# The head of a fused layer norm, S5 and GEGLU kernel: one tile leads the layer norm, weights arrive in other chunks on one queue, and TensorE gets dummies in between

## The chip, the cores and the metric

The kernel runs on one core of a Trainium2 chip. The metric is device time in microseconds (us).

## The reference

The input is normalised without a learned scale, then goes through two branches in parallel: a diagonal state space (S5) with a skip, and a GEGLU feed-forward. Input, branches and skip are added.

```python
B, S, D, F, P = 1, 2048, 512, 1376, 512          # bf16 inputs and output
xn = (x - mean(x)) / sqrt(var(x) + 1e-5)
# branch A: h[t] = Lam_bar * h[t-1] + B_bar @ xn[t] (complex, 512 states);  y = 2 Re(C h) + xn * Dskip
# branch B: (gelu(xn @ w_gate) * (xn @ w_up)) @ w_down
return x + A(xn) + B(xn)
```

## The kernel before

The 2048 tokens are four blocks (0 to 3) of four tiles of 128 tokens. The feed-forward's 1376 hidden columns are eleven column tiles (ten of 128, one of 96). The program is a list of operations with the buffers they read and write. A list scheduler fixes each engine's order from estimated durations and inserts semaphore waits; TensorE and the SyncE queue keep the order in which the operations were written. A change of an estimate can thus reorder VectorE and ScalarE anywhere.

Five names recur. `LN` normalises (VectorE, with a small Sqrt on ScalarE in block 0). `TR0` transposes a tile of block 0 on TensorE through PSUM and evicts it. `GU` is gate and up. `BU` is the state input. `DN` is the output product.

```python
nwarm = 11                                    # dummies: 128x512 matmuls on zeros, so that the array comes to full clock
PE(fwarm, ...)
LN(0, [0, 1], True)                           # tiles 0 and 1 as a pair
TR0(0, "AV")                                  # two transposes evicted by ScalarE, two by VectorE
TR0(1, "V", ...)
LN(0, [2, 3], True, ...)
load_B()
GU_first(range(5), range(3), hbanks)          # gate/up of column tiles 0..4 on block 0, piece by piece
...
BU(0); CHAIN(0, 2); SKIP(0); LN(1); SKIP(1); TR(1); load_C()
GU(0, [5, 10, 6, 7, 8, 9])
# ... blocks 1 to 3 likewise, then DN(2), DN(3)

FCH = [(0, 384), (384, 896), (896, F)]        # weight chunks: 3, 4 and 4 column tiles
for j in range(4): ld_x0(j)                   # SyncE queue
ld_w(WG, ..., 0, "scalar")                    # w_gate chunk 0, ScalarE queue
ld_w(WU, ..., 0); ld_w(WG, ..., 1); ld_w(WU, ..., 1)

# GU_first, TensorE order: early = column tiles 0, 1, 2
for n in (1, 0):
    for ft in early: mm(ft, 0, 0, 1, [2*n, 2*n+1], ...)   # gate, tile 0, 128 columns a matmul
for ft in early: mm(ft, 1, 0, 1)                          # up, tile 0
params()                                                   # one tiny transpose
for ft in early:
    for u in range(2): mm(ft, u, 1, 2)                    # gate and up, tile 1
mm(late[0], 0, 0, 2)                                      # gate of column tile 3, tiles 0 and 1: 256 columns
TR0(2, "V"); TR0(3, "A")
# ... evictions; gate of column tile 4, up of 3 and 4 (256 columns); then tiles 2 and 3 of all five
```

## Time and profile before

| | before |
|---|---|
| time, median | 179.52 us (3 runs, 179.49 to 179.67) |
| execution of the profile | 179.44 us, span 177.6 |
| TensorE, VectorE, ScalarE busy | 98%, 88%, 52% |
| first gate matmul | 6.45 us |
| first matmul of BU(0) | 16.10 us in the list; 16.26 on the chain, behind the end of GU |
| end of the last matmul | 175.35 us |

From the page of before: the span, the busy time of each engine, the granted clock of TensorE in 40 slices, and the shares of the chain of work that ended last.

```profile
span 177.6 us, 2525 instructions
...
PE 173.5 (98%) x927; PEld 86.4 (49%) x927; DVE 156.3 (88%) x275; ACT 91.5 (52%) x175; POOL 10.1 (6%) x20
...
PEclk9999999999999999999999999999999999999999
...
PE 95%; DVE 2%; DMA 1%; issue 0%; ACT 0%; ACTq 0%; DVEq 0%
```

The PEclk row is what a throttle grants.

The same chain in order of time (start, length, what), for its first 16 us:

```profile
2.87 1.29 DVE arena L603 x2
...
5.11 0.42 DVE arena L615
...
5.58 0.41 PE PS L640 x4
...
6.45 0.83 PE PS L729 x12
7.28 0.03 issue
7.30 0.84 PE PS L729 x12
...
16.26 6.91 PE PS L667 x32
```

After 6.45 us the chain is matmuls. The 3.6 us from the arrival of tile 0 to the first gate matmul are the only long stretch in which another engine decides.

The timeline restricted to TensorE's matmuls (start, length, line, how many; merged when back to back). L889 are dummies, L640 transposes, L729 the first gate and up, L537 the tiny transpose, L667 BU.

```profile
0.99 3.88 PE L889 MATMUL PS<-arena 128*128 128x512 bf16 x11 [0.99 <-DVE arena L515]
5.58 0.72 PE L640 MATMUL PS<-arena 128*128 128x128 bf16 x8 [0.70 <-DVE arena L615]
6.45 1.70 PE L729 MATMUL PS<-arena 128*128 128x128 bf16 x24
8.08 0.18 PE L537 MATMUL PS<-arena 12*128 12x12 bf16 x1
8.19 1.95 PE L729 MATMUL PS<-arena 128*128 128x128 bf16 x28
9.98 0.61 PE L640 MATMUL PS<-arena 128*128 128x128 bf16 x8
10.42 5.84 PE L729 MATMUL PS<-arena 128*128 128x256 bf16 x52
16.10 7.07 PE L667 MATMUL PS<-arena 128*128 128x512 bf16 x32
```

The same for weight loads, one ahead of each matmul. Their spacing shows the array's clock:

```profile
3.10 0.15 PEld L889 LDWEIGHTS PS<-arena 128*128 128x128 bf16 x1 [0.28 <-issue]
3.52 0.15 PEld L889 LDWEIGHTS PS<-arena 128*128 128x128 bf16 x1 [0.28 <-issue]
3.85 0.53 PEld L889 LDWEIGHTS PS<-arena 128*128 128x128 bf16 x3 [0.17 <-issue]
...
7.30 0.67 PEld L729 LDWEIGHTS PS<-arena 128*128 128x128 bf16 x12 [0.20 <-DMA arena<-in_B_w_up_dram]
```

Up to 3.52 the loads are 0.43 us apart, then 0.21: the array came to full clock near 3.7 us in this execution. At 7.30 the load waited for the first chunk of w_up.

### The profile page before, as it was taken

Reading aid. Unit: us, or ns where it says so; the run is one execution under the profiler, and the core shown is the slowest. Engines: PE = TensorE matmul, PEld = TensorE weight load, DVE = VectorE, ACT = ScalarE, POOL = GpSimd, SP = SyncE. Lnnn points to the kernel's source line nnn. Section 1 sums busy time; section 2 is a strip of 40 time slices with the busy share of each in tenths; the row PEclk is TensorE's granted clock in tenths of the full one; section 3 lists DMA queues with packets and bytes.
Section 4 is the critical chain, followed back from the end, with each engine's and each line's share of the span. In section 5 each row is a group of like instructions: output and inputs, shape, how many; then the busy total and the mean of one; then the engine's idle time right before and its main releaser. Section 6 shows DMA issues by size and latency. Waiting matters only on the chain.

```text
span 177.6 us, 2525 instructions
## 1 busy us (share of the span) xinstructions
PE 173.5 (98%) x927; PEld 86.4 (49%) x927; DVE 156.3 (88%) x275; ACT 91.5 (52%) x175; POOL 10.1 (6%) x20
## 2 busy tenths in 40 slices
PE   7899999999999999999999999999999999999994
PEld 2597464444644444444644444444464444444453
DVE  5759997998998999779999999999999999999311
ACT  3289999976766899002576495000658700620000
POOL 3120025000000002400000000000000000000000
PEclk9999999999999999999999999999999999999999
DMA  4999914999043000001015000000001000002211
GB/s 132 336 302 163 327 26 95 194 159 339 13 86 61 4 0 0 0 30 63 30 33 113 3 6 0 30 30 30 30 4 30 0 0 0 0 0 78 73 50 39
DMA packets 26387, 12.90 MB, mean 73 GB/s; under 512 B 17704, under 2 KB 26376, under 8 KB 26376
## 3 DMA queue, kind: packets, MB, share of 16 engines
q1 hardware_dynamic: 25824, 12.36, 28.3%
q10 hardware_dynamic: 552, 0.40, 0.9%
q8 instruction: 7, 0.11, 0.3%
q14 instruction: 4, 0.03, 0.1%
HBM read 6.46 MB, written 2.10 MB: 48 GB/s over the span
## 4 chain that ended last, share of the span: by engine, by line
PE 95%; DVE 2%; DMA 1%; issue 0%; ACT 0%; ACTq 0%; DVEq 0%
PE PS L846 37%; PE PS L806 34%; PE PS L667 16%; PE PS L729 5%; PE PS L780 3%; DMA arena<-in_A_x_dram 1%; DVE arena L603 1%; PE PS L640 0%; DVE arena L615 0%; ACT arena L607 0%; DVE arena L649 0%; DVE arena L864 0%; DVE arena L604 0%; DVE arena L611 0%; PE PS L537 0%
## 5 line engine op out<-in xcount | busy, mean ns | idle before, releaser
L846 PE MATMUL PS<-arena 128*128 128x512 bf16 (+3 forms) x323 | 66.2, 366 | 0.0
L806 PE MATMUL PS<-arena 128*128 128x512 bf16 x280 | 61.7, 379 | 0.0
L846 PEld LDWEIGHTS PS<-arena 128*128 128x128 bf16 (+1 forms) x323 | 30.8, 98 | 35.2
L821 ACT ACTIVATE arena<-PS 128x512 bf16<-128x512 f32 x35 | 20.8, 598 | 46.4 <-PE PS L806 33.0
L806 PEld LDWEIGHTS PS<-arena 128*128 128x128 bf16 x280 | 27.3, 98 | 32.1
L700 DVE TENSOR_TENSOR_SCAN arena<-arena 128x512 bf16<-128x512 f32 x32 | 38.8, 1253 | 0.0
L667 PE MATMUL PS<-arena 128*128 128x512 bf16 x128 | 28.3, 379 | 0.0
L824 ACT ACTIVATE arena<-PS 128x512 bf16<-128x512 f32 x35 | 20.8, 597 | 4.9 <-PE PS L806 4.9
L667 PEld LDWEIGHTS PS<-arena 128*128 128x128 bf16 x128 | 12.5, 98 | 14.9
L864 DVE TENSOR_TENSOR arena<-PS,arena 128x512 bf16<-128x512 f32 (+2 forms) x17 | 10.9, 651 | 9.6 <-PE PS L846 9.6
L671 ACT ACTIVATE arena<-PS 128x512 bf16<-128x512 f32 x32 | 17.7, 597 | 3.0 <-PE PS L667 2.9
L826 DVE TENSOR_TENSOR arena<-arena 128x512 bf16<-128x512 bf16 x35 | 13.7, 416 | 2.9 <-ACT arena L824 2.9
L838 ACT ACTIVATE PS<-arena 128x512 f32<-128x512 bf16 (+2 forms) x17 | 9.6, 581 | 5.5 <-DVE arena L864 4.8
L603 DVE BATCH_NORM_STATS2 arena<-arena 128x6 f32<-128x512 bf16 x16 | 10.1, 680 | 1.2 <-DMA arena<-in_A_x_dram 1.1
L729 PE MATMUL PS<-arena 128*128 128x256 bf16 (+1 forms) x104 | 9.5, 248 | 0.2
L687 DVE TENSOR_TENSOR arena<-arena 128x4096 bf16<-128x4096 bf16 (+1 forms) x5 | 9.3, 1857 | 0.0
L689 DVE TENSOR_TENSOR arena<-arena 128x4096 bf16<-128x4096 bf16 (+1 forms) x5 | 9.3, 1856 | 0.0
L712 DVE TENSOR_TENSOR arena<-arena 128x4096 bf16<-128x4096 bf16 x4 | 9.1, 2286 | 0.0
L713 DVE TENSOR_TENSOR arena<-arena 128x4096 bf16<-128x4096 bf16 x4 | 9.1, 2286 | 0.0
L729 PEld LDWEIGHTS PS<-arena 128*128 128x128 bf16 x104 | 8.1, 98 | 1.1 <-issue 0.3
L622 DVE TENSOR_TENSOR arena<-arena 128x512 bf16<-128x512 bf16 x16 | 6.0, 414 | 0.0
L780 PE MATMUL PS<-arena 128*128 128x192 bf16 x64 | 5.9, 246 | 0.0
(84 smaller groups left out, 106.5 us busy)
## 6 DMA issues: line engine op xcount, KB each, us to landing
out_dram<-arena SPq DMA_DIRECT2D x15, 128.0 KB, 1.7
arena<-in_A_x_dram SPq DMA_DIRECT2D x3, 512.0 KB, 7.3
arena<-in_B_w_down_dram SPq DMA_DIRECT2D x1, 1280.0 KB, 6.9
arena<-in_A_x_dram SPq DMA_DIRECT2D x4, 128.0 KB, 3.0
arena<-in_B_w_gate_dram SPq DMA_DIRECT2D x1, 512.0 KB, 6.1
arena<-in_B_w_up_dram SPq DMA_DIRECT2D x1, 512.0 KB, 7.0
arena<-in_B_w_gate_dram SPq DMA_DIRECT2D x1, 480.0 KB, 4.4
arena<-in_B_w_up_dram SPq DMA_DIRECT2D x1, 480.0 KB, 5.6
```

The lines of the kernel that those rows point to most:

```text
L603: V(lambda e, tt=tt: e.bn_stats(ST[tt].ap, X[tt].ap), d_dve_1x(512), [X[tt]], [ST[tt]], "bnst", after)
L667: ins_ = e.matmul(PS[bank][:, :], BBT[c][dk].ap[:, 128 * s:128 * (s + 1)], XNT[b].ap[:, dk, :], start=(dk == 0), stop=(dk == KD - 1))
L671: ACT(lambda e, bank=bank, k3=k3, s=s, c=c: e.activation(SSc[k3][s][c].ap, PS[bank][:, :], ACTF.Copy), d_act(512), [BANK[bank]], [SSc[k3][ ...
L700: V(lambda e, g=g, rb=rb, init=init: e.tensor_tensor_scan(g.ap, rb, g.ap, init, ALU.mult, ALU.add), d_dve_scan(512), [g, PA[RRr]] + ([CARc ...
L729: ins_ = e.matmul(PS[bank][:, q0:q0 + 128 * (j1 - j0)], W.ap[:, dk, 128 * ft:128 * (ft + 1)], XNT[0].ap[:, dk, 128 * j0:128 * j1], start=( ...
L780: ins_ = e.matmul(dst, XNT[b].ap[:, dk, 128 * j:128 * (j + 1)], WGU[:, :, dk, f0:f0 + m], start=(dk == 0), stop=(dk == KD - 1))
L806: ins_ = e.matmul(PS[bank][0:m, c0:c1], W.ap[:, dk, 128 * ft:128 * ft + m], XNT[b].ap[:, dk, c0:c1], start=(dk == 0), stop=(dk == KD - 1))
L821: GATE["last_gelu"] = ACT(lambda e, bg=bg, kk=kk, m=m: e.activation(GG[kk].ap[0:m, :], PS[bg][0:m, :], ACTF.Gelu_apprx_tanh), d_act(512), ...
L824: ACT(lambda e, bu=bu, kk=kk, m=m: e.activation(UPB[kk].ap[0:m, :], PS[bu][0:m, :], ACTF.Copy), d_act(512), [BANK[bu]], [UPB[kk]], "evU")
L826: V(lambda e, kk=kk, m=m, ft=ft, k2=k2: e.tensor_tensor(HTt[k2][ft].ap[0:m, :], GG[kk].ap[0:m, :], UPB[kk].ap[0:m, :], ALU.mult), d_dve_tt ...
L846: ins_ = e.matmul(PS[bank][:, c0:c1], l_[:, 128 * j:128 * (j + 1)], r_[:, c0:c1], start=False, stop=last and n == len(ops) - 1, skip_group ...
L864: V(lambda e: e.tensor_tensor(OUTB[ko].ap[:, c0:c1], PS[bank][:, c0:c1], XD[tt].ap[:, c0:c1], ALU.add), d_dve_1x(c1 - c0), [BANK[bank], XD ...
```

## The change

The intent is to start real TensorE work earlier and keep it fed. Tile 0 is normalised ahead of tile 1, and three small dummies fill the gap between their transposes. The weight chunks are 3, 2 and 6 column tiles, all on the SyncE queue in the order of need. The up of column tiles 0 to 2 waits until tile 1 is there and runs in 256-column matmuls. The last evictions of GU_first let VectorE read PSUM. Block 1's LN goes in pairs. The last DN does the hidden products of two tiles ahead of the states. The scheduler gets other estimates. The core of the diff:

```diff
-        FCH = [(0, 384), (384, 896), (896, F)]
+        FCH = [(0, 384), (384, 640), (640, F)]
...
-        for j in range(4):
-            ld_x0(j)
-        ld_w(WG, WGc, ins["B_w_gate"], 0, "scalar").nb = 900.0
+        ld_x0(0)
+        ld_x0(1)
+        ld_w(WG, WGc, ins["B_w_gate"], 0)
+        S.dma(... X_all.ap[:, 2:4, :] ...)          # tiles 2 and 3 in one transfer
         ld_w(WU, WUc, ins["B_w_up"], 0)
...
-        wchunk = lambda ft: 0 if ft < 3 else (1 if ft < 7 else 2)
+        wchunk = lambda ft: 0 if ft < 3 else (1 if ft < 5 else 2)
...
+        def LN_first():                              # fixed VectorE order, one tile at a time
+            for step, j in ((stats, 0), (aggr, 0), (stats, 1), (recip, 0), (aggr, 1), (norm, 0), (recip, 1), (norm, 1)):
+                step(j)
...
+                if h and ft >= 3:                    # VectorE multiplies straight from PSUM
+                    up, rd, dur = PS[bank][:, 256:512], BANK[bank], d_dve_1x(256)
...
-            for n in (1, 0):
+            for n in range(2):
                 for ft in early:
-                    mm(ft, 0, 0, 1, [2 * n, 2 * n + 1], 2, 1, [XT0h[n]])
+                    mm(ft, 0, 0, 1, [2 * n, 2 * n + 1], toks=[XT0h[n]])
             for ft in early:
-                mm(ft, 1, 0, 1)
+                mm(ft, 0, 1, 2)
             params()
             for ft in early:
-                for u in range(2):
-                    mm(ft, u, 1, 2)
+                mm(ft, 1, 0, 2)
             late = [ft for ft in fts if ft not in early]
-            mm(late[0], 0, 0, 2)
+            for ft in late:
+                mm(ft, 0, 0, 2)
             TR0(2, "V")
             TR0(3, "A")
...
+            elif tail:                               # DN(3)
+                for j in range(2):
+                    seed(j); hidden(j)
+                for j in range(2):
+                    states(j); store(j)
...
-        nwarm = 11
+        nwarm = 10
...
-        LN(0, [0, 1], True)
-        TR0(0, "AV")
+        LN_first()
+        TR0(0, "AA")
+        fill(3)
...
-        LN(1); SKIP(1)
+        LN(1, [0, 1]); LN(1, [2, 3]); SKIP(1)
```

More of the change, by code (lines that the diff above doesn't have):

```diff
@@ L16 @@
 SELF_LAT = 40.0
-LAT = lambda d, op: SYNC_LAT if d.kind == "dma" or d.eng != op.eng else (0.0 if d.eng == "tensor" else SELF_LAT)
+LAT = lambda d, op: SYNC_LAT if d.kind == "dma" or d.eng != op.eng else (0.0 if d.eng == "tensor" or d is op.behind else SELF_LAT)
 DMA_ISSUE = 500.0
@@ L63 @@
     __slots__ = ("id", "eng", "fn", "dur", "deps", "kind", "reads", "writes", "start", "finish",
-                 "sem", "val", "users", "tag", "issue", "nb")
+                 "sem", "val", "users", "tag", "issue", "nb", "behind")
     def __init__(self, id_, eng, fn, dur, kind, reads, writes, tag):
@@ L74, in __init__ @@
         self.nb = 0.0
+        self.behind = None
 class Sched:
@@ L125, in dma, with order_behind @@
             self.out_ops.append(op)
+        return op
+    def order_behind(self, op, prev):
+        if prev is not None and prev not in op.deps:
+            op.behind = prev
+            op.deps.append(prev)
+            prev.users.append(op)
         return op
@@ L268, in _forward @@
                 xfer = op.dur - 2000.0
-                t0 = max(st, dma_pipe)
-                dma_pipe = t0 + xfer
+                t0 = max(st, dma_pipe) if xfer > 10.0 else st
+                dma_pipe = max(dma_pipe, t0 + xfer)
                 op.finish = t0 + xfer + 2000.0
@@ L308, in emit @@
                 for d in op.deps:
-                    if d.kind == "eng" and d.eng == e and e == "tensor":
+                    if d.kind == "eng" and d.eng == e and (e == "tensor" or d is op.behind):
                         continue
@@ L471, in ld_x0 @@
             S.dma(lambda e, j=j: e.dma_start(X[j].ap, x2[128 * j:128 * (j + 1), :]), 128 * 1024, writes=[X[j]], tag="ld_x0")
-        for j in range(4):
-            ld_x0(j)
-        ld_w(WG, WGc, ins["B_w_gate"], 0, "scalar").nb = 900.0
+        ld_x0(0)
+        ld_x0(1)
+        ld_w(WG, WGc, ins["B_w_gate"], 0)
+        S.dma(lambda e: e.dma_start(X_all.ap[:, 2:4, :], x2[256:512, :].rearrange("(j p) d -> p j d", p=128)),
+              256 * 1024, writes=X[2:4], tag="ld_x0")
         ld_w(WU, WUc, ins["B_w_up"], 0)
@@ L477, in build @@
         ld_w(WU, WUc, ins["B_w_up"], 1)
-        for q, nm in enumerate(("A_log_dt", "A_Lambda_re", "A_Lambda_im")):
+        for q, (nm, nb) in enumerate((("A_log_dt", 0.0), ("A_Lambda_re", 500.0), ("A_Lambda_im", 1000.0))):
             S.dma(lambda e, q=q, nm=nm: e.dma_start(PROW.ap[4 * q:4 * q + 4, :], ins[nm].rearrange("(s p) -> s p", p=128)),
-                  1024, writes=[PROWq[q]], tag="ld_" + nm, queue="scalar")
+                  1024, writes=[PROWq[q]], tag="ld_" + nm, queue="scalar").nb = nb
         def late_loads():
@@ L519, in build @@
         SCR = A.alloc("SCR", [1], F32)
-        ACT(lambda e: e.activation(SCR.ap, HALF.ap[:, 0:1], ACTF.Sqrt), 200, [HALF], [SCR], "sqrt0").nb = 1900.0
+        ACT(lambda e: e.activation(SCR.ap, HALF.ap[:, 0:1], ACTF.Sqrt), 200, [HALF], [SCR], "sqrt0").nb = 1600.0
         POOL(lambda e: e.memset(HR.ap, 0.0), 300, [], HRp, "hr0")
@@ L582, in build, with tables_dve @@
         K1s, F1s = ring(K1, "K1", KP), ring(F1, "F1", KP)
-        def tables_dve():
+        def tables_dve(behind):
             for s in range(KP):
@@ L589, in tables_dve @@
                   d_dve_1x(512), [IOTJ, W16p[0], K1s[s]], [F1s[s]], "f1")
-            V(lambda e: e.tensor_scalar(A1.ap.bitcast(I32), F1.ap.bitcast(I32), 0x7FFFFFFF, None, ALU.bitwise_and), d_dve_ts4x(2048) * 2, F1s, [A1], "a1")
+            S.order_behind(V(lambda e: e.tensor_scalar(A1.ap.bitcast(I32), F1.ap.bitcast(I32), 0x7FFFFFFF, None, ALU.bitwise_and), d_dve_ts4x(2048) * 2, F1s, [A1], "a1"), behind)
         def tables_act(after_gelu):
@@ L595, in tables_act, with dve, stats, aggr @@
             return ACT(lambda e: e.activation(SINT.ap, F1.ap, ACTF.Sin, scale=-SIN_SCALE), d_act(2048), [F1], [SINT], "sint", after=[t])
+        def LN_first():
+            mvs = [MVt[0][j] for j in range(2)]
+            mns, qbs, rqs = ([cols(t, 0, j, j + 1) for j in range(2)] for t in (MN, QB, RQ))
+            last = [None]
+            def dve(*args):
+                last[0] = S.order_behind(V(*args), last[0])
+            def stats(j):
+                dve(lambda e: e.bn_stats(ST[j].ap, X[j].ap), d_dve_1x(512), [X[j]], [ST[j]], "bnst")
+            def aggr(j):
+                dve(lambda e: e.bn_aggr(mvs[j].ap, ST[j].ap), D_TINY, [ST[j]], [mvs[j]], "bnag")
+                POOL(lambda e: e.tensor_copy(mns[j].ap, mvs[j].ap[:, 0:1]), 200, [mvs[j]], [mns[j]], "mn")
+                ACT(lambda e: e.activation(qbs[j].ap, mvs[j].ap[:, 1:2], ACTF.Sqrt, bias=EPS.ap), d_act(4),
+                    [mvs[j], EPS, SCR], [qbs[j]], "sqrt")
+            def recip(j):
+                dve(lambda e: e.reciprocal(rqs[j].ap, qbs[j].ap), 150, [qbs[j]], [rqs[j]], "rq")
+            def norm(j):
+                dve(lambda e: e.tensor_scalar(XN[j].ap, X[j].ap, mns[j].ap, rqs[j].ap, ALU.subtract, ALU.mult),
+                    d_dve_ts4x(512), [X[j], mns[j], rqs[j]], [XN[j]], "ln_n")
+            for step, j in ((stats, 0), (aggr, 0), (stats, 1), (recip, 0), (aggr, 1), (norm, 0), (recip, 1), (norm, 1)):
+                step(j)
         def LN(b, js=range(4), on_act=False, after=()):
@@ L606, in LN @@
             if on_act:
-                ACT(lambda e: e.activation(qb.ap, mv.ap[:, :, 1], ACTF.Sqrt, bias=EPS.ap), d_act(4), [mv, EPS, SCR], [qb], "sqrt")
+                GATE["sqrt"] = ACT(lambda e: e.activation(qb.ap, mv.ap[:, :, 1], ACTF.Sqrt, bias=EPS.ap), d_act(4),
+                                   [mv, EPS, SCR], [qb], "sqrt")
             else:
@@ L611, in LN @@
             V(lambda e: e.reciprocal(rq.ap, qb.ap), 150, [qb], [rq], "rq")
+            last = None
             for j in js:
@@ L614, in LN @@
                 xs = XN[tt % 8]
-                V(lambda e, tt=tt, j=j, xs=xs: e.tensor_scalar(
+                last = S.order_behind(V(lambda e, tt=tt, j=j, xs=xs: e.tensor_scalar(
                     xs.ap, X[tt].ap, mn.ap[:, j - j0:j - j0 + 1], rq.ap[:, j - j0:j - j0 + 1], ALU.subtract, ALU.mult),
-                  d_dve_ts4x(512), [X[tt], mn, rq], [xs], "ln_n")
+                  d_dve_ts4x(512), [X[tt], mn, rq], [xs], "ln_n"), last)
+            return last
         def SKIP(b):
@@ L656, in TR @@
                     XNT[b].ap[:, :, 128 * j:128 * (j + 1)], XN[tt % 8].ap),
-                    1.2 * 128 * 1024, reads=[XN[tt % 8]], writes=[XTk[b][j]], tag="tr_x%d" % b)
+                    3.0 * 128 * 1024, reads=[XN[tt % 8]], writes=[XTk[b][j]], tag="tr_x%d" % b, issue=1280.0)
         def BU(b):
@@ L719, in GU_first, with mm @@
         def GU_first(fts, early, banks):
-            def mm(ft, u, j0, j1, dks=range(KD), first=0, last=KD - 1, toks=None):
+            def mm(ft, u, j0, j1, dks=range(KD), toks=None):
                 W, Wc = ((WG, WGc), (WU, WUc))[u]
@@ L729, in f @@
                         ins_ = e.matmul(PS[bank][:, q0:q0 + 128 * (j1 - j0)], W.ap[:, dk, 128 * ft:128 * (ft + 1)],
-                                        XNT[0].ap[:, dk, 128 * j0:128 * j1], start=(dk == first), stop=(dk == last))
+                                        XNT[0].ap[:, dk, 128 * j0:128 * j1], start=(dk == 0), stop=(dk == KD - 1))
                     return ins_
@@ L738, in evac @@
                                         d_act(256), [BANK[bank]], [GG[kk]], "gelu", after)
-                ACT(lambda e: e.activation(UPB[kk].ap[:, 0:256], PS[bank][:, 256:512], ACTF.Copy),
-                    d_act(256), [BANK[bank]], [UPB[kk]], "evU")
-                V(lambda e: e.tensor_tensor(HTt[0][ft].ap[:, c0:c0 + 256], GG[kk].ap[:, 0:256], UPB[kk].ap[:, 0:256], ALU.mult),
-                  d_dve_tt2x(256), [GG[kk], UPB[kk]], [HTt[0][ft]], "hmul")
-            for n in (1, 0):
+                if h and ft >= 3:
+                    up, rd, dur = PS[bank][:, 256:512], BANK[bank], d_dve_1x(256)
+                else:
+                    ACT(lambda e: e.activation(UPB[kk].ap[:, 0:256], PS[bank][:, 256:512], ACTF.Copy),
+                        d_act(256), [BANK[bank]], [UPB[kk]], "evU", [GATE["sqrt"]])
+                    up, rd, dur = UPB[kk].ap[:, 0:256], UPB[kk], d_dve_tt2x(256)
+                V(lambda e: e.tensor_tensor(HTt[0][ft].ap[:, c0:c0 + 256], GG[kk].ap[:, 0:256], up, ALU.mult),
+                  dur, [GG[kk], rd], [HTt[0][ft]], "hmul")
+            for n in range(2):
                 for ft in early:
-                    mm(ft, 0, 0, 1, [2 * n, 2 * n + 1], 2, 1, [XT0h[n]])
+                    mm(ft, 0, 0, 1, [2 * n, 2 * n + 1], toks=[XT0h[n]])
             for ft in early:
-                mm(ft, 1, 0, 1)
+                mm(ft, 0, 1, 2)
             params()
             for ft in early:
-                for u in range(2):
-                    mm(ft, u, 1, 2)
+                mm(ft, 1, 0, 2)
             late = [ft for ft in fts if ft not in early]
-            mm(late[0], 0, 0, 2)
+            for ft in late:
+                mm(ft, 0, 0, 2)
             TR0(2, "V")
@@ L758, in GU_first @@
                 evac(ft, 0, [GATE["evTA"]])
-            for ft in late[1:]:
-                mm(ft, 0, 0, 2)
             for ft in late:
@@ L873, in DN @@
                     states(j); store(j)
+            elif tail:
[3 more added lines that the diff above has]
+                    states(j); store(j)
+                seed(2); hidden(2); states(2); store(2)
+                parts = ((0, tail), (tail, D))
+                for c in parts:
+                    seed(3, *c)
+                for c in parts:
+                    hidden(3, *c); states(3, *c); store(3, *c)
             else:
                 for j in range(4):
-                    parts = ((0, D),) if tail is None or j < 3 else ((0, tail), (tail, D))
-                    for c in parts:
-                        seed(j, *c)
-                    for c in parts:
-                        hidden(j, *c); states(j, *c); store(j, *c)
-        nwarm = 11
+                    seed(j); hidden(j); states(j); store(j)
+        nwarm = 10
         wrm4 = WRM.ap.unsqueeze(1).broadcast_to([128, 4, 128])
@@ L906, in build @@
         GU_first(range(5), range(3), hbanks)
-        tables_dve()
+        tables_dve(None)
         GATE["before_gelu"] = [tables_act([GATE["last_gelu"]])]
```

## The prediction

> **What bounds the kernel now.** TensorE. The page gives PE 98% busy; the chain of waits is PE work for 95% of the span and names almost nothing but matmuls from 6.45 us to 175.35. The list of PE waits has two, both before 5.6 us. The clock is full in every slice. So time can be won only before 6.45 us, from inefficient matmuls just after, or from the tail (175.35 to 177.6), which the change leaves. From 16.26 us on there are 159.1 us of dense matmuls that nothing here shortens.
>
> **Head before (chain of waits).** Tile 0 of x lands at 2.85; statistics of both tiles 2.87 to 4.16, aggregation to 4.39, Sqrt 4.50 to 4.80, reciprocal to 5.01, normalisation from 5.11 (0.37 a tile), first transposes 5.58, eviction 6.01 to 6.31, first gate matmul 6.45.
>
> **What the change does.**
> 1. Tile 0 alone: one statistics (0.65) and aggregation (0.15) end near 3.7. Tile 1's statistics cover the Sqrt. Tile 0 is normalised near 5.0 instead of 5.53, tile 1 only near 5.65 (before 5.85). PE order still puts tile 1's transposes ahead of the first gate matmul, and tile 0's evictions go to ScalarE in series (0.38 each). First gate matmul about 5.95: 0.5 us won, less than a whole statistics pass.
> 2. Up of the first three column tiles in 256-column form. By the timeline 128-column matmuls run at 60 to 65 ns, 256-column ones at 109 (52 in 5.68 us). 24 narrow ones (1.5 us) become 12 wide ones (1.3): 0.2 to 0.3 us.
> 3. PE's weight load waited for w_up chunk 0, landing at 7.25. Now it is needed 24 matmuls later: 0.1 us.
> 4. Chunks of 3, 2, 6: w_gate 0 is still issued near 1.6, behind 256 KB of x, and should land before 5.8. 512 KB fewer precede B_re, whose landing (4.87 + 10.6 = 15.5) is only 0.8 us ahead of its use at 16.26, so the gain need not become a wait. The last chunk still has as many bytes before it: w_up landed near 21.2, use near 23.
> 5. Two ScalarE copies (0.4 to 0.5 each) go; VectorE reads PSUM instead. ScalarE is 96% busy between 23 and 33 us and frees the banks that PE reuses at 29.7 only 0.3 us ahead; this should shift it about 1 us earlier. LN of block 1 in pairs: transposes issue from 24.9, needed at 33.1; protection only.
> 6. DN(3): two tiles' hidden products first. CHAIN(3) ends at 160.44, its use was near 161.2. Protection, no gain.
> 7. Ten warm matmuls, not eleven. The Trainium skill, "TensorE: Matmul & The Clock Gate", Part 1, has the array at half clock until about 3.4 us of activity. The trace agrees: weight loads are 0.43 us apart until about 3.9, then 0.22. The dropped one is fast and off the chain.
>
> **Sum.** 0.5 + 0.3 + 0.1 = 0.9 us, all on the chain, if nothing new waits. Predicted 178.6 us, range 178.1 to 179.3. Faster by over 2%: 1%; within: 98%; slower: 1%.
>
> **What would show it.** First gate matmul near 5.95 (right) or still near 6.4; BU(0) beginning near 15.3; no PE wait after it; again 159.1 us of matmuls from there; last matmul ending near 174.5; same tail.
>
> **What would make it wrong.** w_gate 0 landing after 6 us; B_re landing no earlier; the third chunk or tiles 2 and 3 of x late (PE wait near 9.8 or 22.4); ScalarE not freeing banks near 29 us; the array back at half clock before the first transposes; VectorE's static order, which shifts everywhere, starving PE later.

## The result, and the profile after

| | before | after |
|---|---|---|
| median of 6 runs | 179.52 us (179.38 to 179.67) | 179.15 us (178.77 to 179.43) |
| ratio of means, 95% | | 0.9978 (0.9963 to 0.9993) |
| execution of the profile | 179.44 | 179.01 |
| first gate matmul | 6.45 us | 6.17 us |
| last eviction begins | 175.37 us | 174.93 us |

Ratios are the mean time of one kernel's runs over that of the other's of the same rounds, so not quite the ratio of the medians quoted. Executions over 1.5% slower than the fastest of the same kernel are left out of the means. Faster, then, but by 0.37 to 0.39 us where 0.9 was predicted; at a margin of 2% the two count as the same, as the prediction gave with 98%. The time lies within the predicted range; the gain falls well short of the forecast. The executions of the changed kernel spread over 0.66 us in this set, against 0.29 for the kernel before. That difference is not established: in the later sets the kernel before spread over 0.39 to 1.15 us too (179.30 to 180.45 in one set of 11).

The page of after, same lines:

```profile
span 177.2 us, 2507 instructions
...
PE 173.1 (98%) x902; PEld 86.6 (49%) x917; DVE 157.0 (89%) x277; ACT 91.2 (51%) x175; POOL 11.4 (6%) x23
...
PE 84%; issue 0%; DVE 0%
```

Some 15 matmul records are missing from this trace (902, beside 917 weight loads), so its chain breaks off at 25.85 us and the 84% is no change of behaviour. The matmuls of after (L937 dummies, L679 transposes, L943 small dummies, L768 first gate and up, L706 BU):

```profile
0.99 4.45 PE L937 MATMUL PS<-arena 128*128 128x512 bf16 x10 [0.99 <-DVE arena L525]
5.23 0.49 PE L679 MATMUL PS<-arena 128*128 128x128 bf16 x4
5.56 0.33 PE L943 MATMUL PS<-arena 128*128 128x128 bf16 x3
5.72 0.39 PE L679 MATMUL PS<-arena 128*128 128x128 bf16 x4
6.17 1.50 PE L768 MATMUL PS<-arena 128*128 128x128 bf16 x24
7.61 0.18 PE L547 MATMUL PS<-arena 12*128 12x12 bf16 x1
7.71 2.36 PE L768 MATMUL PS<-arena 128*128 128x256 bf16 x20
9.91 0.61 PE L679 MATMUL PS<-arena 128*128 128x128 bf16 x8
10.36 5.47 PE L768 MATMUL PS<-arena 128*128 128x256 bf16 x48
15.88 6.85 PE L706 MATMUL PS<-arena 128*128 128x512 bf16 x31
```

Ten dummies here take longer (4.45 us) than eleven did before (3.88). The weight loads show why:

```profile
4.38 0.15 PEld L937 LDWEIGHTS PS<-arena 128*128 128x128 bf16 x1 [0.28 <-issue]
4.94 0.10 PEld L679 LDWEIGHTS PS<-arena 128*128 128x128 bf16 x1 [0.41 <-DVE arena L628]
5.23 0.32 PEld L679 LDWEIGHTS PS<-arena 128*128 128x128 bf16 x3 [0.19 <-issue]
5.50 0.21 PEld L943 LDWEIGHTS PS<-arena 128*128 128x128 bf16 x3
...
10.30 0.81 PEld L768 LDWEIGHTS PS<-arena 128*128 128x128 bf16 x8
11.27 0.78 PEld L768 LDWEIGHTS PS<-arena 128*128 128x128 bf16 x8 [0.16 <-issue]
```

In this execution all dummy loads are 0.43 us apart to the end, and the spacing drops only near 5.4 us. Tile 0 was normalised at 4.88 (predicted: near 5.0), and the first load for its transposes came at 4.94. The matmul then waited until 5.23 for the tenth dummy to end. So the predicted lead was there, and 0.29 us of it was spent behind dummies on a half-clock array.

From the first gate matmul on, the trace shows no matmul waiting for another engine by name. At the end the lead over before (175.37 - 174.93 = 0.44 us) is what it was at BU(0), whose first weight load came at 15.99 before and 15.55 after. Nothing after 16 us gives or takes anything. The whole question lies in the first 16 us.

### The profile page after: what moved, and what is told of

Its sections match the earlier page's. It is cut to its first block, busy times and chain, and to the rows that moved or that the text cites. A ratio compares the mean times of both kernels' runs of the same rounds, so it can differ in the third digit from the quotient of the medians.

```text
span 177.2 us, 2507 instructions
## 1 busy us (share of the span) xinstructions
PE 173.1 (98%) x902; PEld 86.6 (49%) x917; DVE 157.0 (89%) x277; ACT 91.2 (51%) x175; POOL 11.4 (6%) x23
## 4 chain that ended last, share of the span: by engine, by line
PE 84%; issue 0%; DVE 0%
PE PS L887 37%; PE PS L847 33%; PE PS L706 12%; PE PS L821 2%; DVE arena L905 0%
## 5 line engine op out<-in xcount | busy, mean ns | idle before, releaser
L847 PE MATMUL PS<-arena 128*128 128x512 bf16 x273 | 60.7, 379 | 0.4
L862 ACT ACTIVATE arena<-PS 128x512 bf16<-128x512 f32 x35 | 21.1, 602 | 35.6 <-PE PS L847 33.9
L706 PE MATMUL PS<-arena 128*128 128x512 bf16 x126 | 28.0, 379 | 0.1
L865 ACT ACTIVATE arena<-PS 128x512 bf16<-128x512 f32 x35 | 21.0, 602 | 5.3 <-PE PS L847 5.3
L706 PEld LDWEIGHTS PS<-arena 128*128 128x128 bf16 x128 | 12.5, 98 | 14.9
L710 ACT ACTIVATE arena<-PS 128x512 bf16<-128x512 f32 x32 | 17.9, 597 | 2.1 <-PE PS L706 2.0
L768 PE MATMUL PS<-arena 128*128 128x256 bf16 (+1 forms) x92 | 9.3, 259 | 0.1
L639 DVE BATCH_NORM_STATS2 arena<-arena 128x6 f32<-128x512 bf16 x14 | 8.9, 679 | 0.1
L768 PEld LDWEIGHTS PS<-arena 128*128 128x128 bf16 x92 | 7.8, 98 | 1.1 <-issue 0.4
L589 DVE SCALAR_TENSOR_TENSOR arena<-arena 128x512 bf16<-128x512 bf16 x8 | 5.5, 742 | 1.2 <-ACT arena L586 1.2
```

Source lines behind the costliest of these rows:

```text
L706: ins_ = e.matmul(PS[bank][:, :], BBT[c][dk].ap[:, 128 * s:128 * (s + 1)], XNT[b].ap[:, dk, :], start=(dk == 0), stop=(dk == KD - 1))
L710: ACT(lambda e, bank=bank, k3=k3, s=s, c=c: e.activation(SSc[k3][s][c].ap, PS[bank][:, :], ACTF.Copy), d_act(512), [BANK[bank]], [SSc[k3][ ...
L768: ins_ = e.matmul(PS[bank][:, q0:q0 + 128 * (j1 - j0)], W.ap[:, dk, 128 * ft:128 * (ft + 1)], XNT[0].ap[:, dk, 128 * j0:128 * j1], start=( ...
L847: ins_ = e.matmul(PS[bank][0:m, c0:c1], W.ap[:, dk, 128 * ft:128 * ft + m], XNT[b].ap[:, dk, c0:c1], start=(dk == 0), stop=(dk == KD - 1))
L862: GATE["last_gelu"] = ACT(lambda e, bg=bg, kk=kk, m=m: e.activation(GG[kk].ap[0:m, :], PS[bg][0:m, :], ACTF.Gelu_apprx_tanh), d_act(512), ...
L865: ACT(lambda e, bu=bu, kk=kk, m=m: e.activation(UPB[kk].ap[0:m, :], PS[bu][0:m, :], ACTF.Copy), d_act(512), [BANK[bu]], [UPB[kk]], "evU")
```

## The experiments

The first four runs set theory 1 against rival 2. Theory 1: the dummies, and the instant at which the array comes to full clock, hold the earlier work. Rival 2: ScalarE's serial evictions and TensorE's order set the first gate matmul, whatever the clock. After the first four runs theory 1 was restated as 1': the change wins 0.6 to 0.7 us where the full clock comes in time; in executions where it comes later, the earlier work is done at half clock. Its rival puts the loss into DMA landings or later waits.

All kernels gave correct results. In the dummy experiments only the emitted count changes and the scheduler's estimate stays, so the order of every other engine is identical.

### The control, fewer dummies, more dummies

`a_ctrl` is the changed kernel itself.

> The changed kernel again, unedited, as control on this chip. Theory 1 (the dummy block at half clock holds TensorE): median near 179.1, a spread of about 0.6 us between executions, and the first transposes start when the tenth dummy ends (5.2 us if weight loads stay 0.43 us apart to the end, earlier if they drop to 0.22), not when tile 0 is normalised (4.88). Rival 2 (the serial ScalarE evictions and tile 1's transposes ahead in TensorE's order set the first gate matmul): first gate matmul near 6.15 whatever the clock does.

Measured: five fast executions, 178.82 to 179.81, median 178.91, mean 179.19; ratio to before 0.9974 (0.9952 to 0.9996). The profiled execution was slow, so its trace is not used, and what was expected of the first transposes and the first gate matmul could not be checked in this run.

```diff
-            for _ in range(nwarm):      # 10
+            for _ in range(8):          # a_w8
+            for _ in range(12):         # a_w12
```

> The changed kernel with 8 warm dummies in place of 10; no other instruction moves. Theory 1: even at half clock the block ends by 0.99 + 8 x 0.427 = 4.4 us, so the first transposes start near 4.94, the first gate matmul at 5.85 to 5.95 (6.17 in the profile of after) and the time falls about 0.25 us below the control; if fewer dummies make the array reach full clock later, part of it is given back as transposes and first gate matmuls 107 ns apart. Rival 2: first gate matmul still near 6.15, time as the control.

Measured: median 178.95, mean 179.02 (control 179.19), ratio to before 0.9965. First transposes at 5.08, first gate matmul at 6.04; the array came to full clock near 5.7, later than in the profile of after. So the hold was gone, but the first transposes and the small dummies ran at half clock, and the first gate matmul came only 0.13 us earlier than in the profile of after; the difference to the control is smaller than the spread.

> The changed kernel with 12 warm dummies: the suspected wait enlarged. Theory 1: in an execution that is at half clock through the block it ends at 6.1 us, the first transposes start there, and the time rises by 0.7 us or so; where the array comes to full clock near 3.9 it ends near 5.0 and almost nothing changes. So the mean is 0.3 to 0.7 above the control. Rival 2: within 0.1 us of the control.

Measured: median 178.95, mean 178.96. This expectation fell: the mean did not rise. In its profile (178.73 us) the full clock came near 3.7 and the first transposes ran at 5.02. It is the changed kernel with an early clock: first gate matmul at 5.91, as predicted (5.95), and not at 6.17.

```profile
5.02 0.40 PE L679 MATMUL PS<-arena 128*128 128x128 bf16 x4
5.91 1.52 PE L768 MATMUL PS<-arena 128*128 128x128 bf16 x24
```

Rival 2, which put it at 6.15 whatever the clock, fell with this profile. The clocks of the other five executions are unknown, so whether this set met early clocks by luck, or whether more dummies bring the clock earlier, is not shown.

```diff
-        nwarm = 11 dummies emitted    # the kernel before
+        8 dummies emitted             # b_w8
```

> The kernel before with 8 dummies in place of 11, nothing else moved. Theory 1: there tile 0 was normalised only at 5.53 and even a half-clock block of 11 ends at 5.69, so at most 0.15 us is to be won and the time stays within 0.1 us of before, if the clock does not come later. Rival 2: no change either; this run tells whether fewer dummies delay the full clock (first transposes or gate matmuls 107 ns apart in the trace, and up to 0.5 us slower).

Measured: 180.93 us, ratio 1.0069 (1.0049 to 1.009), 1.3 us slower than before by the means. The expectation "within 0.1" fell, and the condition in it ("if the clock does not come later") is what failed: in its profile, loads stayed 107 ns apart through all 24 first gate and up matmuls, and the spacing halved only near 10.3 us. Eight dummies ended at 4.58 us and the first transposes came at 5.55, a gap of 0.97 us. All six executions were long (180.44 to 181.53). Eight dummies in the changed kernel, with a gap of 0.50, did no such harm. That the gap is the cause is likely, not shown: no run varied the gap alone. (In that profile w_gate also landed late: 0.45 us of waiting at 6.76.)

### A start delay that puts the full clock first

To take the clock out, both kernels got a fixed delay ahead of their loads, and 31 dummies. Times are 6 us longer; only differences count.

```diff
+ VectorE: nine statistics of a scratch tile, then a semaphore (about 6 us in all)
+ SyncE and ScalarE: wait for that semaphore before their first instruction
- TensorE: 10 or 11 dummies
+ TensorE: 15 dummies, wait for that semaphore, 16 dummies
```

> The kernel before with a fixed start delay of about 6 us (nine statistics of a scratch tile on VectorE, for which the DMA queues wait) and 31 dummies on TensorE, 15 ahead of the delay's end and 16 behind it, so that the array is at full clock before tile 0 arrives[...]. Times are about 6 us longer; only the difference of the two delayed kernels counts. Theory 1' (the change does win about 0.7 us where the array is at full clock in time; in executions where it comes later, earlier work is done at half clock and part of the gain goes): the spread of both delayed kernels is small (0.2 us) and after-delayed is 0.65 to 0.75 us below before-delayed. Rival (the loss lies elsewhere, in DMA landings or later waits, not in the clock): difference still near 0.4 and the spread of after-delayed still near 0.6 us.

> The changed kernel with the same delay and the same 31 dummies. Theory 1': 0.65 to 0.75 us below before-delayed, spread 0.2 us; first gate matmul about 0.55 us earlier after the issue of x than in before-delayed, BU(0) about 0.7 earlier. Rival: 0.4 us, spread 0.6.

Measured:

| | median | range | first gate matmul | BU(0) | last eviction begins |
|---|---|---|---|---|---|
| before, delayed (`d_before`) | 185.74 (5) | 185.56 to 185.87 | 12.58 | 22.04 | 181.31 |
| after, delayed (`d_after`) | 185.11 (4) | 185.08 to 185.14 | 12.06 | 21.57 | 180.84 |

The means differ by 185.73 - 185.11 = 0.62 us, a shade under the expected 0.65 to 0.75, and the changed kernel's spread shrinks from 0.66 us to 0.06. The kernel before keeps 0.31 (0.2 was expected), against 1.15 without the delay in the same rounds. Here are the first gate matmuls in both TensorE timelines, of before-delayed:

```profile
12.58 1.51 PE L745 MATMUL PS<-arena 128*128 128x128 bf16 x24 [0.15 <-DVE arena L665]
...
14.13 1.95 PE L745 MATMUL PS<-arena 128*128 128x128 bf16 x28
15.92 0.61 PE L656 MATMUL PS<-arena 128*128 128x128 bf16 x8
```

and of after-delayed:

```profile
12.06 1.53 PE L784 MATMUL PS<-arena 128*128 128x128 bf16 x24
...
13.63 2.36 PE L784 MATMUL PS<-arena 128*128 128x256 bf16 x20
15.82 0.61 PE L695 MATMUL PS<-arena 128*128 128x128 bf16 x8
```

The lead at the first gate matmul is 0.52 us, just what the prediction gave the first step. By BU(0) it is 0.47, where the expectation had 0.7: the rest of GU_first, predicted to add 0.3 to 0.4, added nothing in this pair. The starts give the rates: 20 matmuls of 256 columns from 13.63 to 15.82 are 109.5 ns each; 24 of 128 and four of 256 from 14.13 to 15.92 leave (1.79 - 0.44) / 24 = 56 ns for a narrow one. Twelve wide ones for 24 narrow ones save 1.35 - 1.31 = 0.04 us. The Trainium skill, "TensorE: Matmul & The Clock Gate", section "Wait — 56ns, not 53.3ns?", gives 55.6 ns from start to start at 128 columns at full clock, and the trace agrees (56 ns).

In the two profiled executions the time differs by 185.56 - 185.09 = 0.47, as the chains do. The other four of before-delayed were up to 0.31 slower than the profiled one. Its profile shows no wait for w_up, while the undelayed profile of before does (0.2 us of weight-load idle). That the others had this wait is likely, but they have no trace.

### One part at a time, with the delay

```diff
-        LN_first()
+        LN(0, [0, 1], True)           # d_nolead
```

> After-delayed with tile 0 and 1 normalised as a pair again (LN(0, [0, 1])), all else as after. If the lead of tile 0 is worth what the prediction said (0.5 us), this is 0.5 us slower than after-delayed, and the first gate matmul comes 0.5 us later. If the gain comes from elsewhere (eviction, clock) it is under 0.2.

Measured: 185.40 (185.38 to 185.45, 4 runs), 0.30 us slower than after-delayed; first gate matmul at 12.53 (0.47 later), last eviction at 181.29 (0.45 later). By the chain the lead is worth what was predicted, and the spans of the two profiles differ by about as much (183.5 and 183.1 us); the time shows 0.15 less. That 0.15 lies outside the profiled span: the time is 1.9 us above the span here and 2.0 in after-delayed. It stays open.

```diff
             for ft in early:
-                mm(ft, 0, 1, 2)
+                mm(ft, 1, 0, 1)
             params()
             for ft in early:
-                mm(ft, 1, 0, 2)
+                mm(ft, 0, 1, 2); mm(ft, 1, 1, 2)      # d_narrow
```

> After-delayed with the up matmuls of the first three column tiles in 128-column form again, in the order of before. The prediction gave 0.2 to 0.3 us for the wide form and 0.1 for the wait on w_up 0, 0.4 together. If narrow ones cost 60 ns and wide ones 109, the form alone is 0.13 us; the up of tile 0 is then needed about 0.7 us after the first gate matmul, and w_up 0 lands about 4.5 us after its issue at x + 2.0, so a wait of 0.1 to 0.3 us may show before it. So 0.13 to 0.4 us slower than after-delayed; under 0.1 would mean that this part was worth nothing.

Measured: 186.33 us, and a spread of 1.0 us (185.80 to 186.80): three times the expected loss. VectorE's and ScalarE's orders moved too in this run, but the list of TensorE's waits names the cause:

```profile
PE PS L784 <- DMA arena<-in_B_w_up_dram: 1.1, 1, 1.1
```

w_up 0 is now issued behind w_gate 0 and tiles 2 and 3 on the one queue, and landed 5.3 us after its issue in this profile (4.5 in after-delayed). In the old order TensorE needs it 12 matmuls after the first gate matmul. So the new TensorE order is worth little against the kernel before, but the new queue order cannot do without it.

```diff
-        FCH = [(0, 384), (384, 640), (640, F)]
+        FCH = [(0, 384), (384, 896), (896, F)]        # d_chunks; wchunk likewise
```

> After-delayed with the weight chunks of before (3, 4 and 4 column tiles), still all on one queue. If the chunk sizes are mere protection: time within 0.1 us of after-delayed (185.11). If they carry the gain: w_gate 1 (512 KB) is needed about 8.1 us after the issue of x and lands about 8.5 after it by the rate of before, so TensorE waits 0.3 us or more before the fourth column tile, and B_re lands 2 to 3 us later, close to BU(0); then 0.3 us or more slower.

Measured: 185.74 us (185.64 to 185.99, 4 runs), 0.63 slower than after-delayed, which ran on another chip and in other rounds: without the small second chunk the gain is gone. The waits of TensorE's weight loads in its profile:

```profile
PEld PS L784 <- DMA arena<-in_B_w_up_dram: 0.6, 1, 0.6
PEld PS L784 <- DMA arena<-in_B_w_gate_dram: 0.2, 1, 0.2
```

The 0.2 is the larger w_gate chunk 1 landing late, as expected. The 0.6 for w_up 0 (landing 5.2 us after issue) was not expected; the next run shows a wait of 0.5 with the small chunk too, so it belongs partly to landings that vary from one execution to the next. Whether the larger chunk behind it slows w_up 0 stays open.

```diff
-            for ft in late:
-                mm(ft, 0, 0, 2)
+            mm(late[0], 0, 0, 2)
             TR0(2, "V")
             TR0(3, "A")
+            mm(late[1], 0, 0, 2)                       # d_late
```

> After-delayed with the gate of the fifth column tile behind the transposes of tiles 2 and 3 again, as before. If the 0.16 us gap before the second-half matmuls (weight loads 16.21 to 17.18, eight of them) is the wait for the ScalarE eviction of tile 3, it goes and the time falls by 0.06 us or so; but tile 2 and 3 are normalised only at 15.30 and 15.66 in after-delayed and their transposes would now be due at 15.28, so if VectorE's statistics bind instead, TensorE waits there 0.1 to 0.2 us and the time rises by up to 0.15.

Measured: 185.03, 185.07, 185.30 and 185.34. The gap before the second-half matmuls is gone from its trace. The profiled execution (185.30) waited 0.5 us for w_up 0, which landed 5.1 us after its issue. The two fastest lie 0.06 under after-delayed by their means (185.05 and 185.11), but on another chip and in other rounds. The traces give the same: from the first gate matmul to BU(0) it takes 9.89 us here, 0.44 of it lost to w_up 0, and 9.51 in after-delayed. The changed kernel thus gave 0.06 us away by drawing four matmuls ahead that had covered the eviction of tile 3. VectorE did not hold the transposes.

### Pairs of clock and time, and a candidate

`a_ctrl2` is the changed kernel again; `a_late12` and `a_late9` have d_late's order with 12 and 9 dummies and no delay; `p_before1`, `p_before2` and `p_after` are the two kernels unedited.

> The changed kernel again as control. Theory 1': executions between about 178.75 and 179.9, median near 179.1; in the profile the time belongs to the instant at which the spacing of TensorE's loads halves: at 3.95 us a time near 178.75, each microsecond that it comes after 5 costs about half a microsecond. Rival: no such relation.

> The changed kernel with 12 dummies and the gate of the fifth column tile behind the transposes: the candidate for a version that beats both. At best 0.1 us below the control, lost in its spread; the same relation of time and clock instant holds, with up to 0.4 us more where the clock comes late, since the longer block then holds the transposes to 6.1.

> The kernel before, one look. Theory 1': with the clock at 3.95 us it took 179.44. If the spacing of the loads halves before 5.7 the time is within 0.15 of that, since eleven dummies at half clock end at 5.69 and the first transposes were due at 5.58; if it halves at 6.5 or 7, between 179.6 and 180.2, with the transposes of tiles 0 and 1 and part of the first gate matmuls 107 ns apart. Rival (no relation to the clock): time and instant unrelated.

> A second look at the kernel before, with the same two expectations as for the first look (p_before1).

> The changed kernel, one look. Pairs so far: clock at about 5.5 us, 179.01; about 6.6, 179.46; and with 12 dummies 3.95, 178.73. Theory 1' puts this look on that line within 0.15 us.

> The changed kernel with 9 dummies and the gate of the fifth column tile behind the transposes. Nine dummies end at 4.83 us even at half clock, so the transposes start at 4.94 in every execution; with the 0.06 us that the delayed kernel showed for the order, 0.1 to 0.2 us below the control's mean (179.18), so 178.95 to 179.1, fastest near 178.7; if the shorter block brings the clock later, no gain.

Measured, profile by profile, the instant of the full clock read from the spacing of the weight loads (0.43 to 0.21 us between dummies, 107 to 56 ns between 128-column matmuls):

| execution | dummies | full clock near | first transposes | first gate matmul | time |
|---|---|---|---|---|---|
| before, first profile | 11 | 3.7 us | 5.58 us | 6.45 us | 179.44 us |
| before, p_before1 | 11 | 4.1 | 5.60 | 6.47 | 179.34 |
| before, p_before2 | 11 | 6.4 to 6.8 | 5.69 | 6.78 | 179.56 |
| changed, a_w12 | 12 | 3.7 | 5.02 | 5.91 | 178.73 |
| changed, p_after | 10 | 5.4 | 5.23 | 6.16 | 178.96 |
| changed, first profile | 10 | 5.4 | 5.23 | 6.17 | 179.01 |
| changed, a_w8 | 8 | 5.7 | 5.08 | 6.04 | 178.86 |
| changed, a_ctrl2 | 10 | 6.9 | 5.23 | 6.40 | 179.46 |
| other order, a_late12 | 12 | 5.5 | 5.77 | 6.61 | 179.38 |
| other order, a_late9 | 9 | 7.0 | 4.95 | 6.10 | 179.27 |

The control set a_ctrl2 had a median of 179.28 (178.83 to 179.46, 5 runs), ratio to before 0.9986 (0.9974 to 0.9998). In p_before2 all eight transposes still ran at half clock, the last at 6.31, and the gate matmuls from 6.78 at full clock; these are its loads:

```profile
5.69 0.77 PEld L640 LDWEIGHTS PS<-arena 128*128 128x128 bf16 x8 [0.74 <-DVE arena L615]
6.75 1.38 PEld L729 LDWEIGHTS PS<-arena 128*128 128x128 bf16 x24 [0.29 <-issue]
```

Here are two weight-load lines of a_ctrl2, the latest clock in the unedited changed kernel: four transposes in 0.47 us and 24 gate loads in 1.65, against 0.27 and 1.35 in the first profile of after.

```profile
5.87 0.47 PEld L679 LDWEIGHTS PS<-arena 128*128 128x128 bf16 x4
6.30 1.65 PEld L768 LDWEIGHTS PS<-arena 128*128 128x128 bf16 x24
```

In the changed kernel three small dummies stand between the transposes of tiles 0 and 1, and in a_ctrl2 TensorE runs from the first transpose to the first gate matmul without a pause; these three take 0.32 us of that (0.17 in the profile of after). In after the first gate matmul came about 0.5 us after ScalarE began its first eviction (5.65 to 6.17); the same lag would give 6.2 in a_ctrl2 (eviction from 5.68), and it came at 6.40. So, by this estimate, they hold up the head by 0.2 us when the clock is late. The prediction does not mention them and no run removes them.

The time follows the clock in these profiles: one execution a row, some with other dummy counts, and from several chips, on which the kernel before had medians of 179.49 to 179.53. Between 3.7 us (with 12 dummies) and 6.9 us the changed kernel loses 0.73 us; the kernel before, between 4.1 and 6.4 to 6.8, loses 0.22. The gain is 0.61 us for an early clock (179.34 to 178.73, with 12 dummies in the latter) and 0.1 for the latest clocks seen of both (6.9, and 6.4 to 6.8). The first look at before and the one at after lie where their expectations put them, within 0.15 us. The second look at before missed narrowly: for a clock at 6.5 it expected at least 179.6, with gate matmuls at half clock, of which there were none.

a_late12 shows the hold by itself. These are the load of the twelfth dummy and those of the first transposes:

```profile
5.23 0.15 PEld L937 LDWEIGHTS PS<-arena 128*128 128x128 bf16 x1 [0.28 <-issue]
5.56 0.43 PEld L679 LDWEIGHTS PS<-arena 128*128 128x128 bf16 x4 [0.17 <-issue]
```

With twelve dummies the first transposes came at 5.77, 0.54 after those of after with ten and the clock at practically the same instant (5.5 and 5.4), and the time was 0.4 us longer in spite of the better order. So more dummies were harmless only where the clock came early: the mean of a_late12 was 179.45 (179.22 for a_ctrl2), ratio 0.9999 (0.9981 to 1.0018), while a_w12 with the same count had 178.96, likely with earlier clocks, of which one is traced.

a_late9, the candidate: 179.03 us (178.75 to 179.27, 5 runs), ratio to before 0.9965 (0.9952 to 0.9979). Its profile had the latest clock of all but b_w8 and was still 0.19 us faster than a_ctrl2. It beats the kernel before. Its mean, 178.99, is below that of the 16 fast runs of the changed kernel in three sets (179.18), as expected, but they did not share rounds and the intervals overlap, so that it beats the changed kernel is likely and not shown.

## Why the prediction was right or wrong

| term | predicted | full clock first (delayed pair) | first profiles |
|---|---|---|---|
| first gate matmul earlier (1) | 0.5 us | 0.52 | 0.28 |
| wide up matmuls (2) | 0.2 to 0.3 | 0.04 | about the same |
| wait on w_up gone (3) | 0.1 | 0 in this pair; up to 0.3 in other runs, likely | 0.1 to 0.2 |
| eviction of tile 3 less covered | not seen | -0.06 | -0.06 |
| sum | 0.9 | 0.47 here, 0.62 by the means | 0.43 |

- **What bounds the kernel: right.** TensorE from the first gate matmul to the end; no stage after 16 us changed by more than the reading error.
- **Step 1: right in mechanism and size, as long as the array is at full clock.** d_nolead and the delayed pair show 0.47 to 0.52 us at the first gate matmul.
- **Step 7 is the step that failed.** It took one profile, in which the clock came at 3.7, for all executions, and concluded that "the dropped one is fast and off the chain". (In that profile the clock came 2.7 us after the first dummy, so "the trace agrees" with 3.4 us is loose too.) In other executions all the dummies run at half clock, and ten of them end at 5.23 us. Before the change the dummies held nothing even then: in p_before2 the transposes began at 5.69, when tile 0 was ready, and running them at half clock cost 0.22 us (1.09 us from there to the first gate matmul, against 0.87 in p_before1). After it, tile 0 is ready at 4.88, so the very gain of step 1 moves work under the dummies and into the half-clock time: 0.73 us between a_w12 and a_ctrl2. Of the 0.62 us that the change is worth with the clock out of the way, 0.37 to 0.39 is left on average. The list of dangers did name "the array back at half clock before the first transposes", but the array had never left it.
- **Step 2 was mis-sized.** The rate of 60 to 65 ns seems to come from lengths of merged rows, which contain the drain and the wait on w_up; that wait was then counted again in step 3. Starts in the same profile of before give 56 ns (8.19 to 9.98), and hence 0.04 us. The sum had 0.3 for this step, so it accounts for about as much of the missing 0.5 us as step 7.
- **Step 3: right in mechanism.** The wait is gone from every profile of the undelayed changed kernel. Its size varies with the landing of w_up 0 (4.4 to 5.3 us after issue), and the delayed kernel can still show it (d_late).
- **Step 4: chunks do keep the gain from becoming a wait, in part as argued.** d_chunks loses 0.63 us, of which 0.2 is the larger w_gate chunk 1; the wait for w_up 0 cannot be put down to the chunks. The prediction named B_re as what would bind; the trace of d_chunks shows no wait for B_re.
- **Steps 5 and 6: no gain, as said.** No wait of that kind shows in either trace. They were not tried apart.
- **Missed: a new wait.** The prediction does not mention it: drawing the last gate matmuls ahead of the transposes left 8 instead of 12 matmuls to cover the eviction of tile 3 (d_late).

What stays open: the split of the remaining 0.25 us between clock and w_up landings in executions without a trace, whether the larger chunk itself delays w_up 0, and what the three small dummies are worth.

## What to carry to other kernels

When a head of a few microseconds is tuned, look at several profiles for the instant at which the array comes to full clock; one profile is one draw. Warm-up dummies stand in TensorE's queue, so choose their count so that they end, at half clock, just before the first real operand is ready, and lower it whenever that operand comes earlier; but too few can leave a gap, and in the one kernel where that gap was 0.97 us the clock came only near 10.3 us (b_w8). That such a count beats the changed kernel is not shown (a_late9). Take rates from starts, never from the lengths of merged rows, and to measure a head by itself, delay it until the clock is out of the question: here that cut the spread from 0.66 us to 0.06.

## What the Trainium skill lacked or had wrong

- "TensorE: Matmul & The Clock Gate", section "What's actually happening", says that the window runs freely and that the cold count varies, and the runs agree that the instant varies: full clock between 3.7 and 7.0 us with dummies from 0.99 us (10.3 in b_w8). Its advice not to fit to a cold count because the ramp is under 1% of a span is right about size (0.73 us of 179 between the earliest and the latest) but hides that this is twice the mean gain of a tuned head.
- The same section gives about 3.4 us of sustained activity; in two profiles the full clock came already 2.7 us after the first dummy (before and a_w12). Neither it nor what the page says of idle gaps gives how much idle time a window may hold while the array is still at half clock. With eight dummies and then 0.97 us without a matmul the full clock came at 10.3 us (180.93 us, b_w8); with 0.50 us, and small dummies between the transposes (a_w8), it came at 5.7.
- No page says that dummies themselves hold the first real matmul: twelve of them, the first ten at half clock, started the transposes at 5.77 us instead of 4.95 (a_late12 and a_late9).
- "DMA: Bandwidth & Descriptors" does not say how much the landing of one transfer varies between executions: w_up 0, 384 KB, landed 4.5 to 5.3 us after its issue behind the same bytes in the changed kernel and its variants, and TensorE waited for it up to 1.1 us (d_narrow).
